# The first five columns of expert 0 as steps of the layer before it

## The chip, the core and the metric

The kernel runs on one core of a Trainium2 chip. The metric is the device time of one execution in microseconds (us); three runs of the kernel before took 809.41, 809.5 and 816.89 us, median 809.5 us.

## What is computed

Three layers follow each other: attention with hashed buckets over 2 x 8 heads of 768 positions, a gated MLP over the 1536 tokens, and a mixture of eight experts in which each token goes to the one expert with the largest logit. The change stands between the second and the third:

```python
def _moe_ref(x, w_gate, w_val, w_out, rms_g):       # second layer: 512 -> 1536 -> 512
    xn = x / sqrt(mean(x * x, -1) + 1e-06) * rms_g
    g = xn @ w_gate
    return (g * sigmoid(g) * (xn @ w_val)) @ w_out
def _moe2_ref(x, w_gate, w_output_gate, w1, w2):    # third layer: 8 experts, 512 -> 1024 -> 512
    logits = x @ w_gate
    e_idx = argmax(logits, axis=1)
    gate_w = softmax(logits)[arange(N), e_idx]
    eom = sigmoid(x @ w_output_gate)
    for e in range(E):
        mask = e_idx == e
        h = maximum(x[mask] @ w1[e], 0.0)
        out[mask] = gate_w[mask, None] * eom[mask, e, None] * (h @ w2[e])
```

Products are made at nearly f32 accuracy from operands split into a high and a low f32r part (hi = cast of x, lo = x - hi); a product is three: hi hi, hi lo, lo hi.

## The kernel before, in words

Up to about 330 us the core computes the attention. Then `first_layer` (L1227) computes the gated MLP in three chunks of 512 tokens (CT = 4 tiles of P = 128). Its work is a list of steps, each with an engine, a cost in ns, a priority (`place`), the steps that it needs and the buffers that it takes and gives (`plan.add`); `Plan.order` plays the list through with these costs, each engine always taking the ready step of smallest priority, and `plan.emit` writes the instructions in that order. So the order of every engine's queue is settled before the program runs. In it: `products` (L934, gate and value products of 128x512), `outp` (L988 to L990, the output products), `y_copy`, `y_store` (L1004, the finished token rows go from `yt` to the DRAM tensor `y_dram`), `y_turn` (L1013, transposes on TensorE), `logits` (L1028), `logits_out` (L1034, `lg`), and the weight casts `wgh`, `wvh`, `woh` on ACT (`split_hi`, L397) with their remainders `wgl`, `wvl`, `wol` on POOL (L953). The last tile's last output product, its transposes and its logits are done in two halves (`M.oq`, `M.yr`, `M.lg` with `hv`).

When a chunk's logits are there it is routed. `route_slots`: the one-hot `oh` of each token's expert (L1068), rank dots `pr` (L1074 to L1078, bf16 products that count the earlier tokens of each expert), `rk` and `rank` (L1087, L1091), the match `ohr` of a token's rank with slot numbers (L1097), the slot dots `pdp` (L1103), which turn it into token numbers, and from these `gid` (L1111) and the running table `disp_i` (L1115); `run`, `pn` and `sn` (L1119 to L1133) carry the counts to the next chunk. `route_gates` (L1148 to L1218: `sh`, `ex`, `se`, `sl`, `ls`, `gd`, `gr`, `g`, `GTS`, `gn`, `movg`, `pdg`, `eo`, `ei`) computes each token's gate. Each expert has 256 slots, two tiles of 128: the ids of the first tile, `gid[0]`, are final after chunk 1 (a count below 128 is padded there, so that chunk 2 fills the second tile alone), and those of the second, `gid[1]`, after chunk 2. In chunk 2 the slot steps have priority 0.0.

Then the experts. `gather` (L1395) reads the token rows of each tile from `y_dram` with an indirect DMA of POOL into `yg`; `to_psum` (L270) turns them on TensorE, and `hi_part` (ACT, `xh`, L273) and `lo_part` (DVE, `xl`, L277) split them. For each of the eight columns f of the hidden width (128 each), `hidden` (L1405) issues twelve products of the column's weights with 256 tokens (L1414), relu (`ehh` on ACT, L1418) and its remainder (`ehl` on DVE, L1419); `second` (L1422) issues six products of 512 columns (L1426 to L1428, three for each tile of tokens), one column behind. `put` scales and scatters the result. The weights come through a ring of slots on the SP queue (`weights`, L1374); expert 0's last three columns wait behind the gather so that its transfer goes first:

```python
    wts = {0: weights(w1[0], w2[0], range(AHEAD))}
    xe = {0: gather(2, [gid[i][:, 0:1] for i in range(2)])}
    wts[0] += weights(w1[0], w2[0], range(AHEAD, NFE), gathers[0])
    for _, _, step in route_gates(NCH - 1):
        step()
```

Of the kernel before, what the change touches and what calls it, by code (L numbers as in the profile page):

```python
# [148 lines left out]
def kernel(  # L149
# [53 lines left out]
    AHEAD = 5  # L203
# [8 lines left out]
    IDS = const.tile([P, NTT, 2], F16, name="IDS")  # L212
# [5 lines left out]
    disp_i = const.tile([P, 2, E, 2], F32, name="disp_i")  # L218
# [16 lines left out]
    def constants():  # L235
# [8 lines left out]
        for b in range(B):  # L244
            iota(IDS[:, b * NT:(b + 1) * NT, 1], [[1, NT]], base=b * S, mult=NT, pool=xz)
        nc.gpsimd.memset(run, 0.0)
# [155 lines left out]
    def attention(ctx, after):  # L402
# [362 lines left out]
        def norm0_sum(i):  # L765
            if i == 0:
# [132 lines left out]
    y_dram = dram.tile([NTOK, DM], F32, name="y_dram")  # L899

# [140 lines left out]
    MI = [P, CT, E, 2]  # L1041
    MG = [P, CT, E, 3]

    def route_slots(c):
# [54 lines left out]
        def slot_dots():  # L1099
            pdp = d["pdp"] = ps_t.tile([P, 2, E, 2], F32, name="pdp", tag="t")  # L1100
# [125 lines left out]

    def first_layer():  # L1227
# [34 lines left out]
        for c in range(NCH):  # L1262
# [44 lines left out]
            for t in range(CT):  # L1307
# [12 lines left out]
                add(SP, 620, ("M.st", c, t), y_store, (c, t), [("M.yt", c, t)], pr, bw=730)  # L1320
# [5 lines left out]
            slots = chain(("M.rs", c), route_slots(c), [("M.lc", c, t) for t in range(CT)] + list(slots), at if c < NCH - 1 else 0.0)  # L1326
            if c < NCH - 1:
# [19 lines left out]
                for i in range(CT):  # L1347
# [7 lines left out]
                    add(DVE, 684, ("M.nl", c + 1, i), lambda i=i, c=c, d=d: norm_lo(c + 1, i, d["pt", i]), (), [("M.nh", c + 1, i)], pr, "", "T")  # L1355
        with tc.manual_schedule():
            plan.emit()
# [31 lines left out]
    gathers = []  # L1389

    def gather(nh, gids):
        x = x_tiles(nh * P)
        yg = wa.tile([P, 2, DM], F32, name="yg", tag="wraw", bufs=3)
        for i in range(nh):
            ins = nc.gpsimd.indirect_dma_start(out=yg[:, i], out_offset=None, in_=y_dram,  # L1395
                                         in_offset=bass.IndirectOffsetOnAxis(ap=gids[i], axis=0),
                                         bounds_check=NTOK - 1, oob_is_err=False)
# [4 lines left out]
        gathers.append(ins.ins.name)  # L1402
        return x

    def hidden(nh, x, r, f):  # L1405
        xh, xl = x
        ah, al = split(r[f][0], "g", nc.gpsimd)
        bh, bl = split(r[f][1], "v", nc.vector)
        ph = gv_bank(nh * P)
        n = 0  # L1410
        for d in range(KD):
            dsl = slice(d * P, (d + 1) * P)
            for w_, x_ in ((ah, xh), (ah, xl), (al, xh)):
                nc.tensor.matmul(ph, w_[:, dsl], x_[:, d], start=n == 0, stop=n == 3 * KD - 1)  # L1414
                n += 1
        hh = wk.tile([P, nh * P], F32R, name="ehh", tag="hh")
        hl = wk.tile([P, nh * P], F32R, name="ehl", tag="hl")
        nc.scalar.activation(hh, ph, AF.Relu)  # L1418
        v_.scalar_tensor_tensor(out=hl, in0=ph, scalar=0.0, in1=r32(hh), op0=ALU.max, op1=ALU.subtract)  # L1419
        return hh, hl, bh, bl  # L1420
# [19 lines left out]
    def run_expert(nh, n0, x, r, gates, sids, between=None, final=False):  # L1440
# [17 lines left out]
        return put(nh, py, gates, sids)  # L1458

# [51 lines left out]
    tail = []  # L1511
    for e in range(E):
        if e + 1 < E:
            wts[e + 1] = weights(w1[e + 1], w2[e + 1])
# [5 lines left out]

        end = run_expert(2, 2 * (e % 2), xe.pop(e), wts.pop(e), [gate[:, i, e:e + 1] for i in range(2)],
# [57 lines left out]
```

## Time and profile before

| | |
|---|---|
| median of the runs | 809.5 us |
| the profiled execution | 814.29 us, of which its span 812.4 us |
| PE (TensorE matmul) busy | 752.3 us, 93% of the span |
| PEld (weight load) busy | 631.3 us, 78% |
| DVE, ACT, POOL busy | 463.7, 373.7, 391.7 us (57%, 46%, 48%) |
| chain of waits, shares of the span | PE 78%, DMA 7%, DVE 6%, issue 3% |
| DMA | 93.88 MB, mean 116 GB/s |

A busy share is a mean over stages with different limits, and the seconds of a stage are read from its own stretch of the trace. The page cuts the span into 40 slices of 20.3 us with a digit each for the busy share of each engine in tenths; the timeline shows the single instructions with their start and duration; the chain of waits is followed back from the last instruction, and shows for each piece of time the one instruction or transfer that the rest waited for. The clock of TensorE that the throttle granted is shown as a share of full speed (2.4 GHz). Matmuls overlap, so that one instruction's duration is longer than the spacing of a series.

### The profile page before, as it was taken

The numbers are of one execution on the slowest core, as the hardware profiler recorded it, in microseconds if no ns is written. First come the engines' busy times: TensorE is split into PE (matmuls) and PEld (weight loads), VectorE is DVE, ScalarE is ACT, GpSimd is POOL, SyncE is SP. The second block draws the span as 40 slices with busy tenths as digits, with TensorE's granted clock in tenths as the row PEclk, the third lists the DMA queues.
The fourth block names the chain that finished last, engine by engine and source line by source line (L and its number), as shares of the span: only waits on it lengthen the run. The fifth ranks groups of instructions, "written<-read, shape, count | busy, mean of one in ns | idle before, by whom it ended". The sixth has DMA issues, their size and how long they took to land.

```text
span 812.4 us, 14342 instructions
## 1 busy us (share of the span) xinstructions
PE 752.3 (93%) x5491; PEld 631.3 (78%) x5491; DVE 463.7 (57%) x856; ACT 373.7 (46%) x620; POOL 391.7 (48%) x314
## 2 busy tenths in 40 slices
PE   5678999999988799999999999999969999999995
PEld 3456778888867668888888888788858888888894
DVE  5665566588769988778756332621253444455441
ACT  3034564445536454444443443443324566655662
POOL 4043576675945224333543343446134666554552
PEclk9698999999999999999999999999988999999998
DMA  8787757563620434454110001020049997768000
GB/s 171 169 166 138 161 115 153 103 126 65 141 65 3 132 102 150 132 158 133 51 52 1 0 1 53 1 65 14 1 154 315 342 308 215 221 183 187 34 24 20
DMA packets 110120, 93.88 MB, mean 116 GB/s; under 512 B 46174, under 2 KB 91326, under 8 KB 110049
## 3 DMA queue, kind: packets, MB, share of 16 engines
q1 hardware_dynamic: 104352, 83.82, 39.9%
q0 software_dynamic: 2560, 7.34, 2.9%
q10 hardware_dynamic: 3136, 1.78, 1.0%
q8 instruction: 44, 0.72, 0.4%
q14 instruction: 28, 0.22, 0.1%
HBM read 66.36 MB, written 7.36 MB: 91 GB/s over the span
## 4 chain that ended last, share of the span: by engine, by line
PE 78%; DMA 7%; DVE 6%; issue 3%; ACT 2%; ACTq 2%; POOL 1%; SPq 0%; POOLq 0%; DVEq 0%
PE pg L934 22%; PE pg L1414 11%; PE pss L646 7%; PE psm L606 4%; PE po L988 4%; PE po L990 4%; PE po L989 4%; PE po L1428 3%; PE po L1426 3%; PE po L1427 3%; DMA T<-HL 3%; DVE m L615 2%; PE po L678 2%; PE po L679 2%; PE po L680 2%
## 5 line engine op out<-in xcount | busy, mean ns | idle before, releaser
L665 POOL TENSOR_TENSOR Pl<-Pe 128x768 f16<-128x768 f32 x90 | 136.3, 1539 | 115.9 <-ACT Pe L654 115.6
L387 POOL TENSOR_TENSOR wgl<-r,wgh 128x512 fp32r<-128x512 f32 x64 | 83.1, 1304 | 80.9 <-ACT wgh L397 76.0
L654 ACT ACTIVATE Pe<-pss,ebias 128x768 f32<-128x768 f32 x96 | 82.8, 898 | 74.7 <-PE pss L646 48.6
L615 DVE TENSOR_REDUCE m<-psm 128x1 f32<-128x768 f32 x96 | 88.8, 949 | 38.1 <-PE psm L606 37.4
L646 PE MATMUL pss<-T 128*128 128x384 f32 x384 | 84.9, 357 | 5.5 <-DMA T<-mT 3.4
L953 POOL TENSOR_TENSOR wol<-wy_o,woh 128x512 fp32r<-128x512 f32 x36 | 49.3, 1371 | 57.9 <-ACT woh L397 57.9
L387 DVE TENSOR_TENSOR wvl<-r,wvh 128x512 fp32r<-128x512 f32 x64 | 49.7, 776 | 48.1 <-ACT wvh L397 41.3
L953 POOL TENSOR_TENSOR wgl<-wy_g,wgh 128x512 fp32r<-128x512 f32 x29 | 39.5, 1360 | 74.4 <-ACT wgh L397 68.1
L1414 PE MATMUL pg<-xh,wgh 128*128 128x256 f32 x256 | 73.5, 288 | 0.7 <-ACT xh L273 0.7
L646 PEld LDWEIGHTS pss<-T 128*128 128x128 f32 x384 | 66.2, 193 | 8.6 <-DVE uT L629 3.7
L1414 PE MATMUL pg<-xh,wgl 128*128 128x256 f32 x256 | 72.8, 284 | 0.0
L1414 PE MATMUL pg<-xl,wgh 128*128 128x256 f32 x256 | 72.8, 284 | 0.0
L606 PE MATMUL psm<-T 128*128 128x384 f32 x192 | 60.4, 409 | 12.2 <-DMA T<-HL 5.9
L966 DVE TENSOR_TENSOR si<-pg,si 128x512 f32<-128x512 f32 x30 | 20.7, 688 | 79.4 <-PE pg L934 77.5
L678 PE MATMUL po<-VS,Pe 128*128 128x65 f16 x576 | 64.3, 198 | 0.0
L679 PE MATMUL po<-VS,Pe 128*128 128x65 f16 x576 | 63.6, 198 | 0.0
L680 PE MATMUL po<-VS,Pl 128*128 128x65 f16 x576 | 63.3, 196 | 0.0
L678 PEld LDWEIGHTS <-Pe 128*128 128x128 bf16 x576 | 53.8, 99 | 11.8 <-issue 11.6
L934 PE MATMUL pg<-xh,wgh 128*128 128x512 f32 x144 | 57.7, 401 | 3.5 <-ACT wgh L397 3.5
L397 ACT CAST wgh<-r 128x512 fp32r<-128x512 f32 x64 | 39.7, 620 | 42.9 <-PE pg L1414 32.2
L953 POOL TENSOR_TENSOR wvl<-wy_v,wvh 128x512 fp32r<-128x512 f32 x29 | 40.0, 1380 | 39.9 <-ACT wvh L397 38.8
L988 PE MATMUL po<-woh,hh 128*128 128x512 f32 (+1 forms) x148 | 58.8, 397 | 0.1
(233 smaller groups left out, 1984.5 us busy)
## 6 DMA issues: line engine op xcount, KB each, us to landing
r<-in_moe_w_dram SPq DMA_DIRECT2D x128, 256.0 KB
T<-HL SPq DMA_DIRECT2D x48, 384.0 KB
wraw<-in_moe_w_gate_dram SPq DMA_DIRECT2D x12, 512.0 KB
wraw<-in_moe_w_val_dram SPq DMA_DIRECT2D x12, 512.0 KB
wraw<-in_moe_w_out_dram SPq DMA_DIRECT2D x12, 512.0 KB
kraw<-in_k_dram SPq DMA_DIRECT2D x16, 192.0 KB
X<-in_v_dram SPq DMA_DIRECT2D x16, 192.0 KB
y_dram<-yt SPq DMA_DIRECT2D x12, 256.0 KB
```

Source lines behind the costliest of these rows:

```text
L387: eng.tensor_tensor(out=lo, in0=y, in1=r32(hi), op=ALU.subtract)
L606: nc.tensor.matmul(pm[:, hf, 0:HS], Tj[:, 0, 1, t * P:(t + 1) * P], Tj[:, 0, 0, hf * HS:(hf + 1) * HS], start=True, stop=True)
L615: v_.tensor_reduce(out=d["m", j][:, t:t + 1], in_=d.pop(("pm", n))[:, :, 0:HS], axis=AX.XY, op=ALU.max)
L646: nc.tensor.matmul(pss[:, hf, 0:HS], Tj[:, a, 0, ks], Tj[:, a, 1, qs], start=a == 0, stop=a == 1)
L654: nc.scalar.activation(d["p", j][0][:, kb], d.pop(("s", n))[:, :, 0:HS], AF.Exp, bias=ebias, scale=1.0 / math.sqrt(D))
L665: eng.tensor_tensor(out=Pl[:, kb], in0=Pe[:, kb].rearrange("p a s -> p (a s)"), in1=leading(Pe, kb), op=ALU.subtract)
L678: nc.tensor.matmul(po, leading(Pe, kb)[:, ts], vf[:, 0], start=t == 0 and kb == 0, stop=False, skip_group_check=True)
L679: nc.tensor.matmul(po, leading(Pe, kb)[:, ts], vf[:, 1], start=False, stop=False, skip_group_check=True)
L934: nc.tensor.matmul(pg, w_[:, dsl], x_[:, d], start=n == 0, stop=n == 3 * KD - 1)
L953: nc.gpsimd.tensor_tensor(out=lo, in0=Y[(f, kind)], in1=r32(hi), op=ALU.subtract)
L988: nc.tensor.matmul(pos[c, t][:, cols], d["hh"][:, tsl], wh[:, cols], start=first, stop=split, skip_group_check=split)
L1414: nc.tensor.matmul(ph, w_[:, dsl], x_[:, d], start=n == 0, stop=n == 3 * KD - 1)
```

## The change

Expert 0's first tile of tokens, whose ids are known after chunk 1, no longer waits for the end of chunk 2.

- The rows of chunks 0 and 1 are stored twice, in `y_dram` and in a new tensor `y_first` of 1024 rows; the first tile of every expert is gathered from `y_first`. IDS gets a third column with the token numbers of that tensor, so `movi` and `pdp` are half as wide again.
- Steps named `E.` join the list of the first layer: five columns of expert 0's weights are loaded during the last part of chunk 2 (`E.ld`, into the buffers `eraw`), cast on ACT (`E.hi`) with remainders on POOL and DVE (`E.lo`), and stay cast; the first tile is gathered (`E.ga`), turned (`E.t`) and split (`E.xh`, `E.xl`).
- The first tile's products for these five columns (`E.x`, two steps of six 128-wide products each; `E.h0`, `E.h1` relu; `E.s`, three second products) are steps with priorities of 99 and more that need the last output product of the layer and the last tile's logits.
- Later `run_first` does the second tile alone for columns 3, 4, 0, 1, 2 (128-wide products), then both tiles for columns 5 to 7. What had waited behind the gather of expert 0, its own last columns, does not; expert 1's weights wait behind the gather of the second tile.

The core of the diff:

```diff
+    y_first = dram.tile([(NCH - 1) * CW, DM], F32, name="y_first")
     def y_store(c, t):
         nc.sync.dma_start(rows_of(y_dram, c * CT + t), yts[c, t])
+        if c < NCH - 1:
+            n = c * CT + t
+            nc.sync.dma_start(y_first[n * P:(n + 1) * P], yts[c, t])
-    MI = [P, CT, E, 2]
+    MI = [P, CT, E, 3]
-                    v_.tensor_tensor(out=gid[i], in0=d["pdp"][:, i, :, 1], in1=disp_i[:, i, :, 1], op=ALU.add)
+                    v_.tensor_tensor(out=gid[i], in0=d["pdp"][:, i, :, 2 - i], in1=disp_i[:, i, :, 2 - i], op=ALU.add)
+    def first_products(ph, a, x, cols, ds):
+        for d in ds:
+            dsl = slice(d * P, (d + 1) * P)
+            for n, (w_, x_) in enumerate(((a[0], x[0]), (a[0], x[1]), (a[1], x[0]))):
+                nc.tensor.matmul(ph, w_[:, dsl], x_[:, d, cols], start=d == 0 and n == 0, stop=d == KD - 1 and n == 2)
+    def e0_lo(f, n):
+        hi, lo = E0["w"][f, n]
+        (v_ if n else nc.gpsimd).tensor_tensor(out=lo, in0=E0["raw"][f][:, n], in1=r32(hi), op=ALU.subtract)
+    def e0_first(f, hv):
+        if hv == 0:
+            E0["p", f] = gv_bank(P)
+        first_products(E0["p", f], E0["w"][f, 0], E0["x"], slice(0, P), range(hv * KD // 2, (hv + 1) * KD // 2))
+    def e0_second(f, m):
+        if f == 0 and m == 0:
+            E0["py"] = out_bank(0)
+        hh, hl = E0["h"][f]
+        bh, bl = E0["w"][f, 1]
+        lhs, rhs = ((hh, bh), (hh, bl), (hl, bh))[m]
+        nc.tensor.matmul(E0["py"], lhs, rhs, start=f == 0 and m == 0, stop=False)
-                add(SP, 620, ("M.st", c, t), y_store, (c, t), [("M.yt", c, t)], pr, bw=730)
+                add(SP, 1240, ("M.st", c, t), y_store, (c, t), [("M.yt", c, t)], pr, bw=1460)
+        for f in range(E0N):
+            pr = at + (3.5 + 0.6 * f if f < E0X else 8 + 0.5 * f)
+            add(SP, 1240, ("E.ld", f), e0_load, (f,), [("M.nl", 2, CT - 1)] + ([("E.ld", f - 1)] if f else []), pr, "WR", bw=1460)
+            for n in range(2):
+                fin = [("M.hi", NCH - 1, NF - 1, "gv"[n])] if f >= E0X else [("M.lo", 2, 4, k) for k in "gv"]
+                add(ACT, 620, ("E.hi", f, n), e0_hi, (f, n), [("E.ld", f)] + fin + ([("E.hi", f - 1, n)] if f else []), pr + 1.4,
+                    ("Wg", "Wv")[n] if f >= E0X else "")
+                add(*((DVE, 690) if n else (POOL, 1303)), ("E.lo", f, n), e0_lo, (f, n), [("E.hi", f, n)], pr + 1.5)
+        add(POOL, 2400, ("E.ga",), e0_gather, (), [("E.ld", E0N - 1)] + [("M.st", 1, t) for t in range(CT)]
+            + ranked, at + 5, "WR", bw=2500)
+        add(PE, 440, ("E.t",), e0_turn, (), [("E.ga",)] + [("M.mm", 1, f, "v") for f in range(NF)], at + 5, "T")
+        for f in range(E0N):
+            pr = 100 + f
+            needs = [("E.xl",), ("E.lo", f, 0), ("M.oq", NCH - 1, lastf, 1), ("M.lc", NCH - 1, 0)]
+            add(PE, 360, ("E.x", f, 0), e0_first, (f, 0), needs, pr, "G")
+            add(PE, 360, ("E.x", f, 1), e0_first, (f, 1), [("E.x", f, 0)], pr - 1)
+            add(ACT, 330, ("E.h0", f), e0_relu, (f,), [("E.x", f, 1)], pr, "HH")
+            add(DVE, 300, ("E.h1", f), e0_rest, (f,), [("E.h0", f)], pr, "", "G")
+            for m in range(3):
+                add(PE, 231, ("E.s", f, m), e0_second, (f, m), [("E.h1", f), ("E.lo", f, 1)] if m == 0 else [("E.s", f, m - 1)],
+                    pr + 1.5 - m, "", "HH" if m == 2 else "")
+    def run_first(r, gates, sids, between):
+        x, py = E0["x"], [E0["py"], out_bank(1)]
+        order = [f for f in range(E0X, E0N)] + [f for f in range(E0X)]
+        for n, f in enumerate(order + list(range(E0N, NFE))):
+            if f < E0N:
+                cur = (f, (1,), n == 0, hidden_of(E0["w"][f, 0], x, slice(P, 2 * P)) + E0["w"][f, 1])
+            else:
+                cur = (f, (0, 1), False, hidden(2, x, r, f))
-    wts = {0: weights(w1[0], w2[0], range(AHEAD))}
-    xe = {0: gather(2, [gid[i][:, 0:1] for i in range(2)])}
-    wts[0] += weights(w1[0], w2[0], range(AHEAD, NFE), gathers[0])
+    wts = {0: [None] * E0N + weights(w1[0], w2[0], range(E0N, NFE))}
+    behind = gather_rows(E0["yg"], 1, y_dram, gid[1][:, 0:1])
-            wts[e + 1] = weights(w1[e + 1], w2[e + 1])
+            wts[e + 1] = weights(w1[e + 1], w2[e + 1], behind=None if e else behind)
```

Line numbers of the changed kernel differ: L1244 are the 128-wide first products, L1305 the second products of the steps, L1253 the relu remainders `ehl`, L1271 the casts of `eraw`, L1110 pdp, L1118 gid, L1094 rk.

How PE's order changes at the last routing. Before, the slot dots follow the rank dots at once (`onesb` and `ohr` are the loaded blocks):

```order
L1078 LDWEIGHTS onesb
L1078 MATMUL pr<-oh,onesb 128x16
L1078 LDWEIGHTS onesb
L1078 MATMUL pr<-oh,onesb 128x8
L1103 LDWEIGHTS ohr
L1103 MATMUL pdp<-movi,ohr 128x16
```

Now, the same place, from the last rank dot on:

```order
L1085 LDWEIGHTS onesb
L1085 MATMUL pr<-oh,onesb 128x8
L1244 MATMUL pg<-xh,wgh 128x128
L1244 MATMUL pg<-xl,wgh 128x128
L1244 MATMUL pg<-xh,wgl 128x128
L1244 MATMUL pg<-xh,wgh 128x128
L1244 MATMUL pg<-xl,wgh 128x128
L1244 MATMUL pg<-xh,wgl 128x128
L1305 MATMUL po_7025<-wvl,ehh 128x512
```

In all 24 such first products and 4 second ones stand between the last rank dot and pdp, and 36 and 4 more ahead of the rank dots, in between the logits; 7 second products stand behind pdp, ahead of the turn of the second tile.

DVE at the last routing, before, from the one-hot's product with IDS to the token ids:

```order
L1082 TENSOR_TENSOR movi<-oh,IDS 128x64
L1160 TENSOR_TENSOR sl<-lg,oh 128x32
L1087 TENSOR_TENSOR rk<-pr,oh 128x32
L1164 TENSOR_REDUCE ls<-sl 128x4
L1210 TENSOR_TENSOR eo<-oh,ecol 128x32
L1091 TENSOR_REDUCE rank<-rk 128x4
L1214 TENSOR_REDUCE ei<-eo 128x4
L1097 TENSOR_SCALAR ohr<-iota_r,rank 128x128 x4
```

Now, the stretch that ends with rank:

```order
L1221 TENSOR_REDUCE ei<-eo 128x4
L1180 TENSOR_SCALAR gd<-en 128x4
L1184 RECIPROCAL gr<-gd 128x8
L1188 TENSOR_TENSOR g<-gr 128x4
L1191 CAST GTS<-g 128x4
L1195 TENSOR_TENSOR gn_7175<-g,GTS 128x4
L1191 CAST GTS<-gn_7175 128x4
L1253 SCALAR_TENSOR_TENSOR ehl<-pg,ehh 128x128
L1094 TENSOR_TENSOR rk<-pr,oh 128x32
L1195 TENSOR_TENSOR gn_7178<-gn_7175,GTS 128x4
L1098 TENSOR_REDUCE rank<-rk 128x4
```

The gate operations, which stood behind the slots, and relu remainders of expert 0 now stand ahead of rk; `movi`, `sl`, `eo` and `ls` stand ahead of these rows, as does `se` (L1163) ahead of oh.

DVE in the routing of chunk 1, which runs beside chunk 2's first products, as it is now:

```order
L1137 TENSOR_REDUCE ot<-oh 128x8
L1271 TENSOR_TENSOR wvl<-eraw,wvh 128x512
L1140 TENSOR_TENSOR run<-run,ot 128x8
L1271 TENSOR_TENSOR wvl<-eraw,wvh 128x512
L1130 TENSOR_SCALAR sn<-pn 1x8
L1133 SCALAR_TENSOR_TENSOR run<-sn,run 1x8
```

The two casts of the expert's weights (wvl) are new between the operations of the chain; a third stands a few rows on, ahead of gd.

## Rows read from the trace of the kernel before

**Rows 1.** The page's 40 slices: TensorE, its granted clock, DMA.

```profile
PE   5678999999988799999999999999969999999995
...
PEclk9698999999999999999999999999988999999998
...
DMA  8787757563620434454110001020049997768000
```

**Rows 2.** Windows: stretch and its length, busy time by engine, granted clock, DMA share, GB/s.

```profile
core 0: us, PE busy (x) PEld busy (x) DVE busy (x) ACT busy (x) POOL busy (x), PEclk, DMA share, GB/s
230.00:231.00 1.00, 1.00 (x23) 0.84 (x24) 0.50 (x1) 0.49 (x1) 1.00 (x1) 0.93 0.00 0
...
234.00:235.00 1.00, 1.00 (x21) 0.76 (x20) 0.43 (x1) 0.00 (x0) 0.00 (x0) 0.86 0.05 16
...
604.00:606.00 2.00, 0.13 (x1) 0.04 (x1) 1.80 (x16) 0.00 (x0) 1.70 (x2) 0.50 0.70 184
612.00:614.00 2.00, 2.00 (x11) 2.00 (x11) 0.18 (x1) 0.06 (x1) 0.58 (x1) 0.50 0.96 241
```

**Rows 3.** The chain of waits from the last routing to expert 1: start, us, what.

```profile
603.47 0.68 PE pdp L1103 x4
...
605.06 3.59 DMA yg<-y_dram,gid
608.79 1.10 PE pt L270 x4
...
610.55 0.80 PE pg L1414 x2
611.54 4.89 PE pg L1414 x22
...
617.95 1.41 PE pg L1414 x12
...
620.76 1.41 PE pg L1414 x12
...
637.35 2.71 PE pg L1414 x23
```

**Rows 4.** Timeline of the last routing: start, us, engine, line, operation, out<-in.

```profile
598.50 0.29 PE L990 MATMUL po<-woh,hl 128*128 128x256 f32 x1
...
601.00 0.17 DVE L1034 COPY lg<-pg 128x16 f32<-128x16 f32 x1 [0.71 <-PE pg L1028]
...
602.10 0.19 DVE L1068 TENSOR_TENSOR oh<-w,mw 128x32 bf16<-128x32 f32 x1
...
602.62 0.19 DVE L1087 TENSOR_TENSOR rk<-pr,oh 128x32 f32<-128x32 f32 x1
...
604.17 0.17 DVE L1111 TENSOR_TENSOR gid<-pdp,disp_i 128x8 int32<-128x8 f32 x1
```

**Rows 5.** Timeline: f32 weight loads and transposes ahead of it.

```profile
595.72 0.60 PE L1013 MATMUL pyt<-ident,yt 128*128 128x128 f32 x4
...
597.10 0.97 PEld L1028 LDWEIGHTS po<-rw,yT 128*128 128x128 f32 x8
...
598.39 0.19 PEld L990 LDWEIGHTS po<-woh,hl 128*128 128x128 f32 x1
```

**Rows 6.** Timeline: a stop of TensorE within the attention.

```profile
229.87 0.59 PE L606 MATMUL psm<-T 128*128 128x384 f32 x2 [2.31 <-DMA T<-bits]
```

**Rows 7.** Timeline: the routing of chunk 1, beside chunk 2's first products.

```profile
517.45 1.13 DVE L1133 TENSOR_TENSOR run<-run,ot 128x8 bf16<-128x8 bf16 x1
...
519.44 0.18 PE L1119 MATMUL pn<-run,onesb 128*128 128x8 bf16 x1
...
527.66 0.26 DVE L1193 TENSOR_TENSOR movg<-oh,GTS 128x96 bf16<-128x96 bf16 x1
...
527.98 0.36 PE L1201 MATMUL pdg<-movg,ohr 128*128 128x24 bf16 x8
```

**Rows 8.** Groups of instructions over the span: count, busy us, mean ns, idle before.

```profile
L387 DVE TENSOR_TENSOR wvl<-r,wvh 128x512 fp32r<-128x512 f32 x64 | 49.7, 776 | 48.1 <-ACT wvh L397 41.3
...
L1013 PE MATMUL pyt<-ident,yt 128*128 128x128 f32 x48 | 7.7, 279 | 0.0
```

More of the change, by code (lines that the diff above doesn't have):

```diff
@@ L202 @@
     TAILF = 4
-    AHEAD = 5
+    E0N, E0X = 5, 3
     v_ = nc.vector
@@ L211 @@
     onesb = const.tile([P, P], BF16, name="onesb")
-    IDS = const.tile([P, NTT, 2], F16, name="IDS")
+    IDS = const.tile([P, NTT, 3], F16, name="IDS")
     GTS = const.tile([P, NTT, 3], BF16, name="GTS")
@@ L1099, in slot_dots @@
         def slot_dots():
-            pdp = d["pdp"] = ps_t.tile([P, 2, E, 2], F32, name="pdp", tag="t")
+            pdp = d["pdp"] = ps_t.tile([P, 2, E, 3], F32, name="pdp", tag="t")
             for i in halves:
@@ new lines, in relu_hi, with relu_lo, e0_load @@
+    def relu_hi(ph, w):
+        hh = wk.tile([P, w], F32R, name="ehh", tag="hh")
+        hl = wk.tile([P, w], F32R, name="ehl", tag="hl")
+        nc.scalar.activation(hh, ph, AF.Relu)
+        return hh, hl
+    def relu_lo(ph, h):
+        v_.scalar_tensor_tensor(out=h[1], in0=ph, scalar=0.0, in1=r32(h[0]), op0=ALU.max, op1=ALU.subtract)
+    E0 = {"w": {}, "raw": {}, "h": {}}
+    def e0_load(f):
+        raw = E0["raw"][f] = wa.tile([P, 2, DM], F32, name="eraw", tag="wraw", bufs=3)
+        nc.sync.dma_start(raw[:, 0].rearrange("p (c w) -> p c w", c=KD),
+                          w1[0].rearrange("(c p) f -> p c f", p=P)[:, :, f * P:(f + 1) * P])
+        nc.sync.dma_start(raw[:, 1], w2[0][f * P:(f + 1) * P])
@@ L1401, in gather, with hidden_of @@
             lo_part(x, i, pt)
-        gathers.append(ins.ins.name)
         return x
     def hidden(nh, x, r, f):
-        xh, xl = x
-        ah, al = split(r[f][0], "g", nc.gpsimd)
+        a = split(r[f][0], "g", nc.gpsimd)
         bh, bl = split(r[f][1], "v", nc.vector)
[L1409 to L1420, printed above, removed]
+        return hidden_of(a, x, slice(0, nh * P)) + (bh, bl)
+    def hidden_of(a, x, cols):
+        w = cols.stop - cols.start
+        ph = gv_bank(w)
+        first_products(ph, a, x, cols, range(KD))
+        h = relu_hi(ph, w)
+        relu_lo(ph, h)
+        return h
     def second(nh, py, f, hs, only=None):
@@ L1458, in run_expert, with second_of @@
         return put(nh, py, gates, sids)
+    def run_first(r, gates, sids, between):
+        x, py = E0["x"], [E0["py"], out_bank(1)]
+        prev = None
+        order = [f for f in range(E0X, E0N)] + [f for f in range(E0X)]
[4 more added lines that the diff above has]
+                cur = (f, (0, 1), False, hidden(2, x, r, f))
+            if prev is not None:
+                second_of(py, *prev)
+            prev = cur
+            if n == 3:
+                between()
+        second_of(py, *prev)
+        return put(2, py, gates, sids)
+    def second_of(py, f, tiles, start, hs):
+        hh, hl, bh, bl = hs
+        for n, i in enumerate(tiles):
+            sl = slice(n * P, (n + 1) * P)
+            nc.tensor.matmul(py[i], hh[:, sl], bh, start=start, stop=False)
+            nc.tensor.matmul(py[i], hh[:, sl], bl, start=False, stop=False)
+            nc.tensor.matmul(py[i], hl[:, sl], bh, start=False, stop=f == NFE - 1)
     first_layer()
@@ L1519, in ahead @@
                 tail.extend(job_list())
+        if e == 0:
+            run_first(wts.pop(0), [gate[:, i, 0:1] for i in range(2)], [sid[:, i, 0:1] for i in range(2)], ahead)
+            continue
         end = run_expert(2, 2 * (e % 2), xe.pop(e), wts.pop(e), [gate[:, i, e:e + 1] for i in range(2)],
```

49 lines of the change are left out of this document (42 added, 7 removed).

## Prediction

> **What bounds the kernel now.** I read the page's forty slices first [rows 1]: PE stands at 9 from the tenth slice to the last but for one slice at 6, the thirtieth (589 to 609 us of 812.4). The whole kernel is a TensorE stream, and the hole between the two layers is the only place left with something to win. The windows [rows 2] show its other half: the granted clock is 0.50 (1.2 of 2.4 GHz) at 604 to 606 and still at 612 to 614, well into expert 0. The chain of waits [rows 3] then tells what sets its end: the slot dots pdp at 603.47, the gather of expert 0 landing at 605.06 + 3.59 = 608.65, its turn at 608.79, the first expert product at 610.55; expert 1's first product is at 637.35. So the price of expert 0 with its hole can be read as one number: when expert 1 starts. From there to the end of the span (812.4 - 637.35 = 175.05 us) the change leaves seven experts as they are, so I move that date and nothing behind it.
>
> A column of F takes 2.81 us warm (617.95 to 620.76), of which twelve first products of 256 columns are 1.41, or 0.1175 each, and six second products the other 1.40, or 0.235 each [rows 3]. Eight columns are 22.5; expert 0 takes 637.35 - 610.55 = 26.80. Of the 4.32 left over, 2.85 is the lower clock: 24 products between 610.55 and 616.43 that would take 2.82 warm took about 5.67 (0.236 each; the granted clock of 612 to 614 in [rows 2]). The rest, 1.47, is the eight transposes of expert 1's tiles (0.86) and 0.6 of small waits.
>
> **The change: what a half-width product costs.** Five columns are split into two 128-wide halves. Second products only change places: three of 0.235 for a tile. The twelve first products of a half, however, each still load 128x128 f32 weights. No row shows such a product, so I bound its spacing u. From below: half of the 256-wide one, 0.059. From above: instructions that load the same f32 block and stream little. Eight logits products of 16 columns have loads that span 0.97 with one load of such a block 0.19, so (0.97 - 0.19)/7 = 0.111 apart [rows 5]; four transposes of 128 columns take 0.60 [rows 5] with one 0.279 [rows 8], so 0.107 apart. The transposes have the same load and the same 128 columns, so I take u = 0.107. Then a half column costs 12 x 0.107 + 0.705 = 1.99 and a split column 3.98 instead of 2.81: the split itself adds 5.8 us of PE time over five columns (nothing if u = 0.059).
>
> The Trainium skill ("TensorE: Matmul & The Clock Gate", section "LDWEIGHTS (loading the stationary operand)") speaks against this change in the same way: a load takes its columns over 1.2 ns, which for 128 is 107 ns whatever streams behind it. The same page's section "Back-to-back issue gap" gives 81 ns for a sustained stream of 128-wide products; by that, an estimate, the split would add 2.7 us, and the forecast below would be near 807.5. No trace of before shows which holds for these operands.
>
> **The first half's place.** Between the last output product (its end 598.79, [rows 4]) and pdp at 603.47 lie 4.68 us, in which PE issues eight logits products (2 x 0.44), two transposes (0.21) and five rank dots (about 0.25): 1.35. So 3.3 us are open there. The order of PE puts 60 half-width products and 8 second products ahead of pdp, the last 24 and 4 of them between the rank dots and pdp: 60 x 0.107 + 8 x 0.235 = 8.30. That overfills the hole by 5.0, so pdp goes to 608.5. DVE is nearly as late. Its routing chain, now at lg 601.00, oh 602.10, rk 602.62, gid 604.17 [rows 4], gets a relu remainder (ehl, 128x128, about 0.3) ahead of lg, another and the sum se, which waits for an exponential behind a table load, ahead of oh, and a dozen gate operations of 0.17 to 0.19 and a third ehl ahead of rk. Step by step: the logits start 0.9 later behind nine products, lg 601.9; to oh the 1.1 of now, the ehl 0.3 and some 0.45 of wait and sum, so 603.75; to rk twelve operations of 0.18 and one ehl of 0.3, so 606.3; from rk to the first product of pdp 0.85 as now, and two operations put between, 0.35: DVE is ready at 607.5, 1.0 ahead of PE. If u is 0.059, PE is ready 2.9 earlier and DVE binds instead.
>
> Then pdp 608.5 + 0.7, gid 609.4, the gather issued at 609.6 (now POOL issues it 0.7 behind gid [rows 3, 4], busy with the tile ahead of it) and landing at 613.2. Behind pdp PE has seven second products (1.65) and stands from 610.9 to 613.3, 2.4 us. From landing to first product is 610.55 - 608.65 = 1.9 now, so 615.1. Then five half columns (9.95) and three whole ones (8.43): 633.5. To this comes the 1.47 of transposes and waits, 0.7 because PE now waits between the second of expert 1's turns and the products around it, with fewer of its own columns to cover it, and the clock. For the clock the nearest row is the attention's stop of 2.31 us ahead of 229.87 [rows 6]: behind it the granted clock was 0.93 over 230 to 231 and 0.86 over 234 to 235 [rows 2], that is 0.50 from about 230.9 to 234.3. I take the same stretch of 3.4 us at half, which costs 1.7 less what falls into the wait for the turn: 1.5 instead of 2.85. Sum: 633.5 + 1.47 + 0.7 + 1.5 = 637.1, against 637.35: **-0.25**.
>
> **What is paid earlier.** (a) In chunk 2 PE turns the first tile there: four transposes, 4 x 0.107 = +0.43. (b) Three casts wvl from the expert's weights stand in DVE's order within chunk 1's routing, each about 0.78 [rows 8]: one ahead of run, one ahead of sn, one ahead of gd. PE waits at two places of this chain. At pn: run ended at 517.45 + 1.13 = 518.58 (an operation on 8 columns that took 1.13 there), pn at 519.44 [rows 7]; 0.86 of slack, about used up by one cast, more if run is slowed again. At pdg: movg ended at 527.92, pdg came at 527.98 [rows 7], so nothing is left over, and the casts delay it by 0.7 to 1.5 less what rearranging gives back. Bounds: 0.43 (all hidden) to 3 (both casts and a slow operation paid); I take **+1.2** in all, near the lower bound since PE has the next column's products behind these. (c) Hidden: eight more stores and ten loads beside a DMA share of 0 to 4 tenths in chunk 2 (the 26th to the 30th slice, [rows 1]); the third column of IDS (movi 96 instead of 64 columns, pdp 24 instead of 16); POOL's four casts and its gather, which take free time between its weight casts, of which it has 1 to 3 us apart; expert 1's weights, which wait for the gather at 613 and are wanted at 637. If POOL's cover were gone, each us of its queue late is a us of PE, see the fourth rival.
>
> **Sum.** -0.25 + 1.2 = +0.95. Profiled execution 814.29 (span 812.4 and 1.9 around it) becomes 815.2; on the median of 809.5, **810.5**. So the forecast is: the hole is filled, and the fill is paid back by the split's weight loads and a gather that starts 4.5 us later.
>
> **Rivals.** A measurement of this kernel can tell about 1% (8.1 us): under 801.4 is faster, over 817.6 slower.
>
> First, the forecast (chance 0.70): 807 to 814.
>
> Second, the gain comes (0.17): half-width products at half price. u = 0.059 takes 2.9 off the fill ahead of pdp, provided DVE keeps up, and 2.9 off the second halves: 804.7; with no clock loss behind a shorter stop 803.2, with chunk 2 at its lower bound 802.4. If the routing were not delayed at all, and nothing lost to the clock, expert 1 would start at 610.1 + 5 x 1.41 + 8.43 + 1.47 + 0.7 = 627.8, 9.6 earlier, less 0.43: 800.3, the ceiling. For it: PE overlaps loads with products elsewhere (PEld is busy beside PE in [rows 2]). Against: the transposes' row, and DVE's order.
>
> Third, slower (0.08): the clock falls within the fill. It is 0.50 at 604 to 606 now; if the waits of the first columns bring that on at 603 as before, the 5 us of PE work then left ahead of pdp double, pdp goes to 613.4, and expert 1 starts 4.9 later: 815.4, or 817 if the second halves begin cold too. It decides if the clock falls more than a us ahead of pdp. Against: PE is busy in most of the stretch in which it now stands.
>
> Fourth, slower (0.05): chunk 2 stalls. If the gather on POOL waits for its ids or stores, the casts queued behind it (wgl, then wvl, wol) are late for the first-layer products, or DVE's casts push pdg by more than a column: from 3 to 8 us, 813 to 818. It decides once POOL stands for more than the 1 to 3 us between its casts. Against: the ids are there when the step is placed.
>
> **Numbers.** Under 801.4 only the ceiling of the second rival: 0.04. Over 817.6 only the ends of the third and fourth: 0.05. Between: 0.91. The range 804.0 to 814.5 leaves out the lower part of the second rival (0.08) and the upper of the third and fourth (0.10).
>
> **What would show it.** In the profile after: the spacing of 128-wide products (0.107, against 0.059); pdp near 608.5 after the fill, with PE and not DVE last ahead of it; a stop of PE of about 2.4 us until the turn of tile 2; a granted clock of 1.00 through the fill and 0.50 for some 3 us behind the stop; expert 1's first product about 1 us later than before, counted with chunk 2's; there the waits at pn and pdg. I am wrong if the spacing is near 0.06, if DVE's chain rather than PE's queue sets pdp, or if the last output product itself comes more than 2 us later.

## The result: about 1.1% slower

Six runs of the changed kernel have a median of 820.5 us against 810.4 before: the ratio is 1.011, with a 95% interval of 1.007 to 1.015. A repetition (819.2 against 810.1, eleven runs of before) gave 1.011 again, 1.007 to 1.014. So the change costs 9 to 10 us, where 1.0 (810.5 on a median of 809.5) was forecast; the time lies outside the range of 804.0 to 814.5. Ratios go by fast executions: one more than 1.5% above the fastest of its kernel (one of `late` at 1057.8 us, one of `warm_late`, five of the ten of `c4f6`) is left out of them.

The profiled execution has a span of 818.4 us against 812.4. The page's slices of the changed kernel, TensorE and its granted clock:

```profile
PE   5778999999988799999999999999999999999995
...
PEclk9698999999999899999999999999995999999998
```

The 6 of the thirtieth slice [rows 1] is gone: the hole between the layers is filled, as the change says. In its place the clock has a slice at 5, from about 614 to 634 us, in which TensorE is busy. The chain of waits (start, us, what) from the gather of the second tile to expert 1:

```profile
611.06 3.56 DMA yg<-y_dram,gid
614.75 0.64 PE pt L273 x4
...
616.06 0.90 PE pg L1244 x3
...
623.25 2.24 PE pg L1244 x11
...
626.88 2.45 PE pg L1244 x12
...
644.02 2.82 PE pg L1244 x24
```

The x24 at 644.02 are expert 1's first products, at 637.35 before [rows 3]. The timeline shows the very first 0.16 earlier in both kernels (643.86 and 637.19); the next table goes by the chain, the one under Experiments and the text behind it by the timeline. The twelve products of a half column take 2.45 us between 616 and 630, and a half column comes every 3.63 (623.25 to 626.88).

Where the 6.0 us of the two profiles are, by stretches (before [rows 3, 4], and the timeline for the rest; its rows of the changed kernel for the gate product, the last output product, pdp and expert 1 follow):

```profile
302.76 0.40 PE L938 MATMUL pg<-xh,wgh 128*128 128x512 f32 x1
...
600.41 0.28 PE L994 MATMUL po<-woh,hl 128*128 128x256 f32 x1
...
610.32 0.27 PE L1110 MATMUL pdp<-movi,ohr 128*128 128x24 f16 x4
...
643.86 0.28 PE L1244 MATMUL pg<-xh,wgh 128*128 128x256 f32 x1
```

| stretch | before | after | difference |
|---|---|---|---|
| start to one gate product of chunk 0 (303.60 and 302.76) | 303.60 | 302.76 | -0.84 |
| that product to the last output product (598.50, 600.41) | 294.90 | 297.65 | +2.75 |
| to pdp (603.47, 610.32) | 4.97 | 9.91 | +4.94 |
| to the landing of the second tile (608.65, 614.62) | 5.18 | 4.30 | -0.88 |
| to the second tile's first product (610.55, 616.06) | 1.90 | 1.44 | -0.46 |
| to expert 1 (637.35, 644.02) | 26.80 | 27.96 | +1.16 |
| to the end (812.4, 818.4) | 175.05 | 174.38 | -0.67 |

The first and the last line are not put down to the change: the first differs by 2.9 us between two profiles of the changed kernel (296.5 to 305.4 over all kernels of this study), the last by 1.1. So kernels are compared below from that gate product on, or by their ratios. (Where the expectations speak of the second layer's first product, `late_again` and `after_again` mean this gate product, the others one 22.7 us later.)

### The profile page after: what moved, and what is told of

The parts are those of the page before. It is cut to its first block, busy times and chain, and to the rows that moved or that the text cites. A ratio compares the mean times of both kernels' runs of the same rounds, so it can differ in the third digit from the quotient of the medians.

```text
span 818.4 us, 14487 instructions
## 1 busy us (share of the span) xinstructions
PE 761.2 (93%) x5551; PEld 640.5 (78%) x5551; DVE 465.7 (57%) x861; ACT 374.5 (46%) x625; POOL 392.3 (48%) x316
## 3 DMA queue, kind: packets, MB, share of 16 engines
q10 hardware_dynamic: 3136, 1.78, 1.0%
## 4 chain that ended last, share of the span: by engine, by line
PE 77%; DVE 8%; DMA 6%; issue 3%; ACT 2%; ACTq 1%; POOL 1%; SPq 0%; POOLq 0%; DVEq 0%
PE pg L938 22%; PE pg L1244 12%; PE pss L649 7%; PE po L992 4%; PE po L994 4%; PE po L993 4%; PE psm L609 3%; PE po L1528 3%; PE po L1527 3%; PE po L1526 3%; DVE m L618 2%; DMA T<-HL 2%; DMA T<-bits 2%; PE po L681 2%; PE po L682 2%
## 5 line engine op out<-in xcount | busy, mean ns | idle before, releaser
L390 POOL TENSOR_TENSOR wgl<-r,wgh 128x512 fp32r<-128x512 f32 x59 | 77.0, 1310 | 61.4 <-ACT wgh L400 61.2
L1244 PE MATMUL pg<-xh,wgh 128*128 128x256 f32 (+1 forms) x276 | 79.7, 290 | 0.7 <-ACT xh L276 0.7
L1244 PE MATMUL pg<-xh,wgl 128*128 128x256 f32 (+1 forms) x276 | 79.6, 288 | 0.0
L1244 PE MATMUL pg<-xl,wgh 128*128 128x256 f32 (+1 forms) x276 | 79.4, 288 | 0.0
L390 DVE TENSOR_TENSOR wvl<-r,wvh 128x512 fp32r<-128x512 f32 x59 | 43.7, 740 | 46.6 <-ACT wvh L400 44.3
L681 PE MATMUL po<-VS,Pe 128*128 128x65 f16 x576 | 63.2, 197 | 0.0
L682 PE MATMUL po<-VS,Pe 128*128 128x65 f16 x576 | 62.5, 196 | 0.0
L1253 DVE SCALAR_TENSOR_TENSOR ehl<-pg,ehh 128x256 fp32r<-128x256 f32 (+1 forms) x69 | 27.9, 405 | 54.5 <-ACT ehh L1249 54.5
```

The lines of the kernel that those rows point to most:

```text
L390: eng.tensor_tensor(out=lo, in0=y, in1=r32(hi), op=ALU.subtract)
L681: nc.tensor.matmul(po, leading(Pe, kb)[:, ts], vf[:, 0], start=t == 0 and kb == 0, stop=False, skip_group_check=True)
L682: nc.tensor.matmul(po, leading(Pe, kb)[:, ts], vf[:, 1], start=False, stop=False, skip_group_check=True)
L1244: nc.tensor.matmul(ph, w_[:, dsl], x_[:, d, cols], start=d == 0 and n == 0, stop=d == KD - 1 and n == 2)
```

## Experiments

All times from a profile are of its own execution. Two stretches carry the readings; both were the same within 0.1 us in two profiles of before and two of after.

| kernel | gate product to last output product | last output product to expert 1 | median us | ratio to before |
|---|---|---|---|---|
| before | 294.90 | 38.69 | 810.4 | |
| after | 297.65 | 43.45 | 820.5 | 1.011 (1.007 to 1.015) |
| warm | 297.66 | 36.36 | 813.0 | 1.002 (1.000 to 1.005) |
| lift | 297.62 | 42.15 | 816.2, one run | |
| late (profile: late_again) | 295.46 | 43.77 | 817.5 | 1.008 (1.005 to 1.011) |
| before_warm | 294.96 | 37.19 | 810.9 | 0.998 (0.996 to 1.000) |
| warm_late | 295.52 | 42.42 | 814.6 | 1.003 (0.999 to 1.006) |
| c5f1 | 295.54 | 34.29 | 806.9 | 0.995 (0.991 to 0.998) |
| c4f6 | 295.50 | 42.13 | 815.0 | 0.997 (0.992 to 1.001), five of ten |
| b4_800 | 295.52 | 41.95 | 814.0 | 1.005 (1.002 to 1.007) |
| best | 295.50 | 33.24 | 805.6 | 0.994 (0.991 to 0.997) |

### Is the profile of before an ordinary one?

The kernel before, unchanged, once more.

> The kernel before, unchanged, profiled once more: the profiled execution of before (814.29 us) lay some 4 us over its median of 810.4, and the shift of the changed kernel is 6.0 us by the two profiles but 10 by the medians. If the 4 us sit in the hole between the layers (a clock that falls in some executions), this profile shows the last output product to expert 1 in less than 38.9 us; if they sit in the attention, that stretch stays at 38.9 and the second layer starts earlier than 326.3.

813.9 us, with 294.95 and 38.70 in the two stretches and the same clock of 0.50. So these stretches repeat, and the low clock behind the last routing belongs to the kernel before as well. Where a median execution saves its 4 us stays open: both profiled executions lie over the median, so neither shows one that takes 810, and the part ahead of the gate product is hardly shorter here (303.12) than in the first (303.60).

### Fill the stop, and nothing else

`warm` adds ten products into an unused bank behind the fill's last second product:

```diff
+    def filler(w, n):
+        scratch = out_bank(3)
+        for i in range(n):
+            nc.tensor.matmul(scratch, w, E0["w"][0, 1][0], start=i == 0, stop=i == n - 1)
+        add(PE, 235 * 10, ("E.fill",), lambda: filler(E0["h"][E0N - 1][1], 10), (), [("E.s", E0N - 1, 2)], 300)
```

> The changed kernel with ten 512-wide products into an unused bank behind the last second product of the fill (ten by 0.235 = 2.35 us), in the stop of 2.4 us ahead of the second tile's turn. Clock theory (the stop brings the clock down, and the half-width products then run at 0.213 instead of 0.111): the granted clock stays 1.00, from the first product of tile 2 to expert 1 takes about 21 instead of 27.8 us, total 813 to 814.5 against 820.5. Rival (the second half's products are slow for another reason, such as weights or casts that come late): still 27 to 28 us, total within 1 us of 820.5.

It takes 813.0, 7.5 us less than the changed kernel. In its timeline the turn of the second tile is where it was, 14.1 us behind the last output product (14.3 in the changed kernel), and behind it only the clock differs. Windows (stretch, its length, busy time by engine, granted clock, DMA share, GB/s) of the changed kernel and then of `warm`:

```profile
614.00:616.00 2.00, 0.63 (x4) 0.42 (x4) 0.00 (x0) 0.58 (x1) 1.00 (x2) 0.83 0.77 199
616.00:618.00 2.00, 1.94 (x12) 1.94 (x13) 1.23 (x4) 0.01 (x1) 1.65 (x2) 0.50 0.81 206
...
630.00:632.00 2.00, 2.00 (x10) 1.70 (x8) 0.00 (x0) 0.39 (x1) 0.00 (x0) 0.50 1.11 331
632.00:634.00 2.00, 1.79 (x15) 1.65 (x14) 0.69 (x1) 0.53 (x2) 0.09 (x1) 0.90 1.11 332
```

```profile
614.00:616.00 2.00, 1.42 (x8) 0.80 (x6) 0.00 (x0) 0.55 (x1) 1.23 (x2) 1.00 0.67 166
616.00:618.00 2.00, 1.73 (x17) 1.67 (x17) 1.23 (x4) 0.04 (x1) 1.68 (x2) 1.00 0.79 213
618.00:620.00 2.00, 2.00 (x18) 1.92 (x17) 0.29 (x1) 1.26 (x3) 0.98 (x1) 1.00 1.03 322
```

In the changed kernel the clock falls in the window that holds the stop and the turn (0.83 over two us: at 0.50 from about 615.3) and is back at 632.4, 17 us later, 16 of them with TensorE at work. In `warm` it stays at 1.00, and the second tile's first product to expert 1 takes 20.9 us (616.09 to 637.01) instead of 27.8 (616.06 to 643.86):

```profile
616.09 0.55 PE L1244 MATMUL pg<-xh,wgh 128*128 128x128 f32 x3 [0.68 <-ACT xh L276]
...
637.01 0.28 PE L1244 MATMUL pg<-xh,wgh 128*128 128x256 f32 x1
```

What this clock does to the narrow products shows in two pairs of the changed kernel's timeline, from the fill and from the second half (start, us, engine, line, operation):

```profile
600.59 0.27 PE L1244 MATMUL pg<-xl,wgh 128*128 128x128 f32 x1
600.70 0.27 PE L1244 MATMUL pg<-xh,wgl 128*128 128x128 f32 x1
...
614.75 0.63 PE L273 MATMUL pt<-ident,yg 128*128 128x128 f32 x4 [2.44 <-DMA yg<-y_dram,gid]
616.06 0.90 PE L1244 MATMUL pg<-xh,wgh 128*128 128x128 f32 x3 [0.67 <-ACT xh L276]
...
617.40 0.41 PE L1244 MATMUL pg<-xh,wgh 128*128 128x128 f32 x1
617.61 0.42 PE L1244 MATMUL pg<-xl,wgh 128*128 128x128 f32 x1
```

0.11 apart in the fill, 0.21 apart behind the stop of 2.44. The second is the spacing that 256-wide products have at this clock in the kernel before: there 22 of them take 4.89 [rows 3], 0.22 each. At the low clock the first products of a half column take as long as those of a whole one; its second products are still half as many.

### What brings the clock back?

`lift` leaves the stop and puts fourteen 512-wide products (into an unused bank) behind the first three narrow ones of the second tile: `filler(x[1][:, 0, P:2 * P], 14)` at the head of `run_first`.

> The changed kernel with fourteen 512-wide products into an unused bank after the first half-width products of tile 2, at the clock of 0.50 some 6 us of wide products. Theory that narrow products, which at the low clock leave the engine loading weights half of the time, keep the clock from rising: it rises to 1.00 within about 7 us of the wide ones, as in the kernel before (610.55 to 616.54), the narrow columns behind them run at 0.111, and expert 1 starts 0 to 2 us earlier than in the changed kernel in spite of the added work. Rival, the low clock lasts some 17 us from its fall whatever runs: it rises no earlier than 632, and expert 1 starts 3 to 6 us later.

```profile
612.00:614.00 2.00, 1.32 (x11) 1.10 (x9) 0.73 (x2) 0.59 (x1) 1.20 (x2) 0.60 0.77 166
614.00:616.00 2.00, 2.00 (x5) 1.57 (x6) 0.50 (x3) 0.00 (x0) 0.80 (x1) 0.50 0.87 278
616.00:618.00 2.00, 2.00 (x6) 1.56 (x5) 0.00 (x0) 0.00 (x0) 0.00 (x0) 0.50 1.06 362
618.00:620.00 2.00, 2.00 (x10) 1.63 (x9) 0.00 (x0) 0.00 (x0) 0.00 (x0) 0.69 1.08 355
620.00:622.00 2.00, 2.00 (x20) 2.00 (x20) 0.27 (x1) 0.80 (x2) 0.39 (x1) 1.00 1.10 330
```

With the wide products, which begin at 613.8, the clock is back at about 619.2, and the narrow ones behind them run at it. Expert 1 starts 42.15 behind the last output product, 1.3 earlier than in the changed kernel, though 5.8 us of useless work were added. So the low clock does not last a fixed time from its fall: behind the stop the engine was busy with half columns (twelve 128-wide products and three 512-wide ones each) for 16 us before it rose, with 512-wide products alone for 5.5, and in the kernel before, with 256-wide ones, for 6.0 (610.55 to about 616.5). That the narrow ones hold it down fits these three, but width alone cannot be it. In the changed kernel the clock rose amid narrow products, ahead of the first 256-wide one. And behind the attention's stop of 2.31 [rows 6], where the clock was back after 3.4 us, most products are narrower still, in another type:

```profile
231.35 0.25 PE L678 MATMUL po<-VS,Pe 128*128 128x65 f16 x1
231.40 0.25 PE L679 MATMUL po<-VS,Pe 128*128 128x65 f16 x1
```

The busy shares do not tell the cases apart either: in both the kernel before (612 to 614, 2.00 of 2.00 us, [rows 2]) and the changed one (616 to 618, 1.94) TensorE and its weight loads are busy nearly throughout. What the throttle counts isn't shown.

### The casts in chunk 1's routing

`late` lets expert 0's first load wait for chunk 1's gates, so its casts come later in the order:

```diff
-            add(SP, 1240, ("E.ld", f), e0_load, (f,), [("M.nl", 2, CT - 1)] + ([("E.ld", f - 1)] if f else []), pr, "WR", bw=1460)
+            add(SP, 1240, ("E.ld", f), e0_load, (f,), [("M.nl", 2, CT - 1)] + list(gates) + ([("E.ld", f - 1)] if f else []), pr, "WR", bw=1460)
```

> The changed kernel with expert 0's loads, and so their casts on POOL and DVE, placed behind chunk 1's routing (one more need on the load step). Theory: the casts between chunk 1's routing operations made TensorE wait 0.5 us at pdp and 1.4 at pn; without them the second layer (first product to last output product) takes 273.1 to 273.5 instead of 275.0, total 818.5 to 819. Rival, the stores or the turn are the cost: it stays at 274.5 to 275.0.

817.5, 3.0 less than the changed kernel; the intervals of the two ratios overlap, so the stretches have to carry the reading. They come from a second profile, `late_again`:

> The kernel late, for one profile (the first was disturbed from end to end). Theory: the second layer takes 295.5 us from its first to its last output product, as in the kernels that contain the same edit, against 297.65 in the changed kernel; the stop and the low clock behind it stay as in the changed kernel, so expert 1 starts 43 us behind the last output product.

295.46 and 43.77: the first stretch is shorter by 2.2, the second not. The changed kernel's timeline around chunk 1's slot dots and counts shows what is gone:

```profile
514.49 1.28 POOL L1271 TENSOR_TENSOR wgl<-eraw,wgh 128x512 fp32r<-128x512 f32 x1 [0.18 <-ACT wgh L400]
514.78 1.66 DVE L1104 TENSOR_SCALAR ohr<-iota_r,rank 128x256 f16<-128x256 f16 x4
...
515.90 0.88 PE L1110 MATMUL pdp<-movi,ohr 128*128 128x24 f16 x8 [0.49 <-DVE ohr L1104]
516.36 1.78 DVE L982 TENSOR_TENSOR hl<-si,hh 128x512 fp32r<-128x512 f32 x1
517.55 3.42 POOL L1271 TENSOR_TENSOR wgl<-eraw,wgh 128x512 fp32r<-128x512 f32 x2
...
518.48 1.36 DVE L1271 TENSOR_TENSOR wvl<-eraw,wvh 128x512 fp32r<-128x512 f32 x1
519.77 1.23 DVE L1140 TENSOR_TENSOR run<-run,ot 128x8 bf16<-128x8 bf16 x1
521.05 0.18 PE L1126 MATMUL pn<-run,onesb 128*128 128x8 bf16 x1 [1.41 <-DVE run L1140]
```

TensorE waits 0.49 at pdp and 1.41 at pn (no wait at either before; pn in [rows 7]). Not only the cast of the weights on DVE (518.48) stands in the chain: the casts on POOL beside it, new in this place, go with DVE operations that last about twice as long as they do elsewhere (hl 1.78; 0.69 in `late_again`, whose POOL does nothing for the expert here; the match 1.66 against 0.88). `late` moves both kinds of cast, so what each costs is not separated. The row of `late_again`:

```profile
512.07 0.69 DVE L982 TENSOR_TENSOR hl<-si,hh 128x512 fp32r<-128x512 f32 x1
```

### The low clock in the kernel before

`before_warm` fills the hole of the kernel before: 36 products of f16 constants around the rank and slot dots, and two f32 ones behind the first tile's turn.

> The kernel before with products into unused banks in the hole between the layers (10 ahead of the rank dots, 6 ahead of pdp, 20 behind it, and 2 behind the first tile's turn), and nothing else changed. Clock theory: the granted clock stays 1.00 through 602 to 617; the turn of tile 2 takes 0.45 instead of 1.10 and the first 24 products of expert 0 2.82 instead of 5.67: expert 1 starts 3.0 to 3.5 us earlier after the last output product than in the kernel before, total near 807. Rival (the low clock has another cause than the standing engine, or the unprofiled runs have none): no change, 810.5.

The clock stayed at 1.00, yet expert 1 starts only 1.5 earlier and the ratio is 0.998, no difference that counts. Two reasons stand in its profile. The two f32 products took 1.9 us and held the first tile's split, so the second tile's turn came 0.7 behind its landing. And the first 24 products of expert 0 take 4.14 at full clock (5.67 before, [rows 3]), not 2.82: among them TensorE stands 0.22 ahead of the gate dots, which take 0.25, and waits 0.48 for a relu that stands behind a weight cast on ACT. So my 2.85 for the low clock in the kernel before was nearly twice what it is, 1.5. The turn of the second tile, behind the wait for that split:

```profile
606.74 0.66 PE L270 MATMUL pt<-ident,yg 128*128 128x128 f32 x4 [0.85 <-DVE xl L277]
```

### Both repairs, and a planner that knows what a step costs

`warm_late` is `warm` with the edit of `late`.

> The changed kernel with both repairs, the ten products in the stop and the expert's loads behind chunk 1's routing. If the two losses are separate they add: 7.6 and 3.1 off 820.5, so 810, level with the kernel before; the second layer takes 273.1 to 273.5 us against 275.0. If the filled stop already hides the routing's waits, 812 to 813.

Here the two do not add: 814.6, between 806.0 and 818.6. The first stretch is short (295.52), but in its profile the clock fell at about 611.8, 17 us behind the last output product, although there was no stop ahead of the turn:

```profile
608.00:610.00 2.00, 1.39 (x8) 0.71 (x6) 0.00 (x0) 0.57 (x1) 1.15 (x2) 1.00 0.71 152
610.00:612.00 2.00, 1.75 (x16) 1.69 (x17) 1.23 (x4) 0.02 (x1) 1.67 (x2) 0.96 0.75 206
612.00:614.00 2.00, 2.00 (x12) 2.00 (x11) 0.29 (x1) 0.79 (x2) 0.78 (x1) 0.50 1.03 334
```

Two waits behind the turn (0.67 for ACT, 0.17 for DVE) and narrow products were all that stood there, and `warm` has the same (0.68 and 0.17) and kept 1.00. The clock came back at about 625.5, 13.7 us later, with nothing but half columns at work and the first of expert 1's turns. The ten products are thus no cure that holds in every execution.

`c5f1` also gives the planner 680 ns for each half-column step (`("E.x", f, 0)` and `("E.x", f, 1)`, 360 in the changed kernel) and only one filling product. 42 narrow products and 4 second ones then stand ahead of pdp instead of 60 and 8; the others come behind it, in the time of the gather:

> As warm_late, with the planner's cost of a half-column step at 680 ns instead of 360 (its measured length is 0.67 us), so that 42 half-width products stand ahead of pdp instead of 60 and the rest behind it; one filling product instead of ten, since the steps now reach to the gather's landing. Theory: of the delay of pdp by 4.9 us about 2.5 go, the stop goes, the clock stays 1.00; expert 1 starts 4 us earlier than in the kernel before, less 0.8 in chunk 2: total 807. Rival (the gather is not what the tail waits for): 810 as warm_late.

pdp comes 7.10 behind the last output product (9.91 in the changed kernel, 4.97 before), TensorE works without a stop until the turn, and the clock stays at 1.00. 806.9, 0.5% less than before, with 1 outside the interval.

`c4f6` is `c5f1` with four columns and six filling products, `b4_800` has four columns, a step of 800 ns and no filling product, and `best` is `c5f1` without its filling product and with expert 1's turns behind the sixth column.

> As c5f1 with four columns in the fill instead of five, and six filling products. One split column less saves 1.25 us of weight loads, and the last column's two halves are one; the gather lands as in c5f1. Theory: within 1 us of c5f1, 807 to 808.

> As c5f1 without its one filling product, and with expert 1's two turns issued behind the sixth column (the first wide one) instead of the fourth. In c5f1 the second of these turns came 2.0 us behind the first with one half-width group of 0.8 us between, so TensorE stood 0.9 there. Theory: that wait goes, expert 1 starts 33.2 to 33.6 us behind the last output product against 34.3, total 806. Rival (the wait is only moved): no change, 807.

> As best with four columns and a modelled step of 800 ns, so that 36 half-width and 3 second products stand ahead of pdp. pdp comes about 0.9 earlier, one split column's 1.25 us are saved, and a stop of about 1 us appears ahead of the second tile's turn. Clock theory: where the stop brings the clock down in an execution, it takes 813 to 818, where it does not, 803 to 806; so a wide spread about 808. Rival (a stop of 1 us is too short to matter): 805 throughout, better than best.

`c4f6` missed its 807 to 808: three of its ten executions took 803.7 to 807.3, seven 813.1 to 820.5. The profiled one (820.5) is among these, with a stop of 0.68 ahead of the turn and the clock at 0.50 from about 615 to 632:

```profile
612.96 0.63 PE L273 MATMUL pt<-ident,yg 128*128 128x128 f32 x4 [0.68 <-DMA yg<-y_dram,gid]
```

Its ratio, over five of the ten, says little about the kernel. `best` takes 805.6, and expert 1 starts 33.24 behind the last output product, the expected 33.2 to 33.6. `b4_800` has the longer stop. Its windows and the timeline's row of its turn, then `best`:

```profile
602.00:604.00 2.00, 0.71 (x5) 0.34 (x4) 0.00 (x0) 0.00 (x0) 1.47 (x2) 1.00 0.71 215
604.00:606.00 2.00, 1.15 (x11) 0.84 (x10) 0.69 (x1) 0.58 (x1) 1.10 (x2) 0.95 0.76 162
606.00:608.00 2.00, 2.00 (x11) 2.00 (x11) 0.54 (x3) 0.00 (x0) 0.89 (x1) 0.50 0.89 298
```

```profile
603.69 0.63 PE L273 MATMUL pt<-ident,yg 128*128 128x128 f32 x4 [1.29 <-DMA yg<-y_dram,gid]
```

```profile
604.00:606.00 2.00, 2.00 (x15) 1.78 (x14) 0.29 (x1) 0.28 (x1) 1.39 (x3) 1.00 0.42 131
606.00:608.00 2.00, 1.32 (x9) 0.87 (x7) 0.08 (x1) 0.59 (x1) 1.16 (x2) 1.00 0.69 172
608.00:610.00 2.00, 1.82 (x18) 1.76 (x19) 1.15 (x4) 0.00 (x0) 1.53 (x2) 1.00 0.89 215
```

The step cost of 800 makes pdp come 0.9 earlier than in `c5f1` (6.18 against 7.10; `c4f6`, with four columns at 680, has 7.09), and the work ends 1.29 us ahead of the gather. Behind this stop of 1.29 and another of 0.67 for the split the clock fell, expert 1 starts 41.95 behind the last output product, and all twelve executions took 811 to 819. The kernel with less to do in the fill is 8 us slower than the one with more.

### The result once more

> The changed kernel itself, with more rounds. The two profiles put the change at 6.9 us between the first product of the second layer and the end, the six runs at 10. The part ahead of the second layer, which the change does not touch, ended between 297.7 and 305.4 us in the profiles so far. If that spread explains the difference, the ratio comes out near 1.0085 and the new profile again shows the clock at 0.50 behind the stop; if the change costs something ahead of the second layer, the ratio stays at 1.011 to 1.012.

The ratio stayed at 1.011 (1.007 to 1.014), and the new profile has the same stretches (297.70, 43.35) and the clock at 0.50 from about 612.6 to 629.7. From the gate product to the end the changed kernel is 6.8 and 7.9 us longer than the kernel before in its two profiles. The 1 to 3 us more that the runs show are not located; they may lie ahead of the second layer, where one kernel varies by about that and where the change adds the third column of IDS.

## Why the prediction was wrong

**The fill's price was right.** 60 products at 0.107 and 8 at 0.235 in an open time of 3.3 were to move pdp by 5.0; it moved by 4.94 (4.97 to 9.91). Narrow products stand 0.11 apart where 0.107 was taken. The Trainium skill's load rule ("TensorE: Matmul & The Clock Gate", section "LDWEIGHTS (loading the stationary operand)", 107 ns for 128 columns) agrees with this; the 81 ns of its section "Back-to-back issue gap" for a sustained stream does not hold for these f32 operands. TensorE's queue, not DVE's chain, set pdp, as forecast.

**The step that failed: the clock behind the stop.** The prediction saw the stop (2.4 us until the turn; measured 2.44) and that the clock would fall there, but took the length of the low clock from the one place in the attention with a like stop, 3.4 us, and so 1.5 us of loss. It lasted 17 us, and cost 6.9: from the second tile's first product to expert 1 27.8 us against 20.9 in `warm`, where I had 22.0 with the 1.5 in it, 20.5 without. So the rest of that sum was right to about half a us, and the clock's term alone was short by 5.4. The row was the wrong one: behind the attention's stop f16 products of 65 columns ran, with a few of 384. The row of the same place, the hole of the kernel before, had the clock at 0.50 at 604 to 606 and still at 612 to 614 [rows 2], and the clock came back after 6 us of 256-wide products; the change puts half columns there, whose first products at this clock cost as much as wide ones, and under which it stayed low for 16.

**The smaller miss: chunk 2.** 1.2 was taken from bounds of 0.43 and 3; it was 2.75, near the upper. One of the prediction's own signs of being wrong, a last output product more than 2 us later, is thus there. The waits came at pn (1.41) and pdp (0.49), where I had looked at pn and pdg; POOL's casts, which I had put down as hidden, stand beside DVE operations of twice their length. With the casts moved away 0.6 is left, about the 0.43 that the turn was put at: the lower bound was right for a change that keeps the routing clear.

**The rest.** The gather landed 4.30 behind pdp (4.7 taken) and its first product followed in 1.44 (1.90): together -0.9. Put into the sum by the chain's rows (27.96 for the 22.0 from the second tile's first product to expert 1), +0.95 becomes 0.95 + 6.0 + 1.55 - 0.1 - 0.9 = 7.5, which is the shift of expert 1 against the gate product in the first table; to the end of the span 6.8 and 7.9 were measured. The first reading of [rows 1], 9 in all slices but one, passes over slices of 8, 8 and 7 in the attention; nothing in the sum rests on it.

**The rivals.** The second, half-width products at half price, fell with the spacing. The third named the right culprit, the clock, at the wrong place: it was to fall in the fill, where TensorE stands no longer; it fell behind it. The fourth, POOL's queue in chunk 2, happened in a milder form. What I lacked is the rival in which the clock's loss is bigger because of what the change puts behind the stop; its price for each product, 0.21 instead of 0.11, could have been worked out from [rows 3] and the spacing, but that it would last for 16 us stood in no row.

## What to carry to other kernels

A filled hole is worth only what the new order of work leaves of it: here the fill doubled the weight loads of five columns' first products, delayed the gather by nearly as much as it saved (with the clock at 1.00 in both, expert 1 starts at 36.36 in `warm` and at 37.19 in `before_warm`) and left a new stop, shorter than the hole but with worse work behind it. Ask of each stop that remains which products follow it: here 256 and 512 columns had TensorE's clock back after 5.5 to 6 us, half columns with f32 weights after 13.7 to 16. And give a planner measured costs: with 0.68 us instead of 0.36 for one kind of step, one more dependency and expert 1's turns two columns later, the same idea is 0.6% faster than the kernel before (`best`) instead of 1.1% slower.

## What was not expected of the hardware

- Behind stops of 1.29 us ahead of the turn and 0.67 behind it the clock fell to 0.50 (`b4_800`, all twelve executions long); with 0.68 and 0.68 it fell in the profile, and seven of ten executions were long (`c4f6`). `best`, `c5f1` and `warm` have only the wait of 0.68 and held 1.00 in their profiles; `warm_late` has no more and fell. Why it fell there is open.
- At the clock of 0.50 128-wide and 256-wide f32r products both stand 0.21 to 0.22 apart; at 1.00 0.111 and 0.1175. Halving the width saves almost nothing at either, for these first products.
- The granted clock stayed low through 16 us of half columns (13.7 in `warm_late`), and rose after 5.5 to 6 us of products of 256 or 512 columns. In the attention it was back after 3.4 us, most of them with 65-column f16 products.
